# A Fourier layer and a mixture of experts on one core: the last-but-one batch's tokens made earlier, and the first head block turned at the last mix

## The chip, the cores and the metric

The kernel runs on one core of one Trainium2 chip. The metric is device microseconds of one execution. Before the change it is 1086.36 us, the median of 3 runs (1083.76, 1086.36 and 1087.21). The engines are named as in the profile: PE multiplies matrices, DVE is the vector engine, ACT the scalar engine, POOL the general engine that also issues the scatters, SP issues the other transfers.

## The reference

```python
X = np.fft.rfft(x, axis=1)                      # x: 8 batches x 2496 x 256
Yr = Xr @ w_r - Xi @ w_i + b_r
Yi = Xr @ w_i + Xi @ w_r + b_i
Y* = sign(Y*) * maximum(abs(Y*) - 0.01, 0)      # soft threshold, both parts
y = np.fft.irfft(Y, n=2496, axis=1)             # 19968 tokens of 256
do = y @ w_skip > 0                             # about half of the tokens
e = argmax(y[do] @ w_gate); g = softmax weight of e     # 8 experts, one each
out = y;  out[do] = y + g * (relu(y @ w1[e]) @ w2[e])   # w1 256x1024, w2 1024x256
```

All of it is in fp32. A product of two fp32 matrices is made as three products of parts (high by high, high by low, low by high), so most tensors exist twice, as a high part from ACT and a low part from DVE or POOL.

## The kernel before

The sequence is split as 39 by 64. A batch is worked off in 20 frequency steps, and the 8 batches make 160 steps in one straight program; every engine runs its instructions in the order in which the code issues them, and nothing else reorders them. Step `i` of the main loop belongs to batch `b` and frequency `k`. In this order it issues:

- `flush_y` and one output unit of the batch before (see below), then the inverse step `inv2_step` of frequency `i-4` (PE `pi`, L606; its copy `g` on ACT);
- the delayed pieces of work that are due at "inv2", and one step of the routing (`run_later`);
- the complex products `mix` (PE `pm`, L570). An odd step ends a pair of frequencies: DVE adds the bias to `pm` (L582), ACT makes `rl` (L584), DVE makes the two `y` (L590) of which the inverse is taken. An even step ends with `mix_sum`, whose products need `fl`, the low part of a sum that POOL makes (L552);
- the delayed work that is due at "sum", and `fwd2_step` for frequency `i+3` (PE `pb`, L536; `fh`, `im`, `fl`, `s`);
- a second output unit in the steps named in `KX` (in the last batch `KX7`), up to two scatters from the list `scq`, loads, and in the last batch a piece of the split of expert 0's weights (`wa2l`, L184).

An output unit makes 117 tokens; a batch has 21 of them, numbered 0 to 20, and besides a few other output tasks (a copy `gq`, a left-over unit, an ending). A unit has a first half, `t` (two transposing matmuls, L620 and L621, then ACT `th` L624 and DVE `tl` L625), and a second half, `y` (three matmuls, L632 to L634, then `row` and `lg` on ACT, L635 and L638). The second half is issued one unit later, by `flush_y`. Seven units are a chunk, and a chunk is followed by a routing of five parts, one part a call of `run_later`: the largest logit and the exponentials; a search for the expert; its one-hot matrix `oh`; a count on PE (`pr`, L675 and L677); and the places `pos` on DVE (L686 to L690). After them seven scatters `xs<-row,pos` of POOL (L693) send the chunk's tokens to the lists of their experts. Batch `b`'s units are made during batch `b+1`. The chunks of batch 6 are numbered 0, 7 and 14 by their first unit and 6, 13 and 20 by their last.

Behind step 159 come four steps (160 to 163) that hold only the last inverse steps, the output units that are left, and one head block task each (`fill.pop`). A head block is a block of 256 tokens of expert 0, from a list that is already full: three of them are worked off while batch 7's tokens are made. A block is loaded as `xg` by SP (L222), turned (`turn`: DVE transpose `hxt<-xg` L229, ACT `bxh` L232, DVE `bxl` L233), then goes through eight `up` tasks (PE `hph`, L241, six matmuls each) and eight `down` tasks (PE `pos`, L254). Then, in the tail, batch 7's own 24 output tasks follow with a head block task behind every third, the first of them `t_0`; SP loads the next expert's weights (`ws`, 2 MB, L172) ahead of it. Behind the tail the experts' loops run to the end.

Of the kernel before, what the change touches and what calls it, by code (L numbers as in the profile page):

```python
# [17 lines left out]
F32 = mybir.dt.float32  # L18
# [8 lines left out]
B, S, D = 8, 2496, 256  # L27
# [9 lines left out]
BLK = 256  # L37
# [3 lines left out]
HEAD = ((3, 6),)  # L41
NHEAD = sum(n for n, _ in HEAD)
D_SUM, D_RELU, D_Y0, D_Y1 = (1, "inv2"), (1, "inv2"), (1, "sum"), (1, "sum")
KX, KX7 = (0, 5, 9, 10, 12, 14, 18, 19), (0, 1, 2, 10, 12, 14, 19)
KA0 = (2, 4, 6, 8)
RK = (13, 15, 18, 3)
WLOAD, WST = (7, 11, 12, 15), (0, 0, 1, 0)
# [119 lines left out]
def load_quarter(nc, a, e, j, st):  # L167

    i, q = divmod(j, 2)
    src = a[("moe_w1", "moe_w2")[i]][e].rearrange("(c p) f -> p c f", p=128)  # L170
    at = (slice(None), slice(q, q + 1) if i == 0 else slice(4 * q, 4 * q + 4))
    nc.sync.dma_start(st.rearrange("p (c f) -> p c f", c=(1, 4)[i]), src[at])  # L172
# [17 lines left out]
def load_expert(nc, a, pool, e):  # L190

    t = pool.tile([128, K1 * D], F32, name=f"ws{e}", tag="g", bufs=2)
    st = [t[:, F * j : F * j + F] for j in range(4)]
    return st, [lambda j=j: load_quarter(nc, a, e, j, st[j]) for j in range(4)]
# [123 lines left out]
def fft_and_route(tc, a, out, zs, xs, kp, pp, keep_, outer):  # L318
# [6 lines left out]
    sp = es.enter_context(tc.tile_pool(name="sp", bufs=2, side="right", reuse_waits="tile"))  # L325
# [479 lines left out]
    def head_tasks(wt, pool):  # L805
        r2 = [sp.tile([128, F // 256, BLK], F32R, name=f"hhl{i}", tag="r", bufs=3) for i in range(2)]
        bk = Blocks(tc, out, xs, ident, pool, None, lambda f: r2[f // 4][:, f % 4, :], pp.tile([128, 2, D], F32, name="pos", tag="pm", bufs=2))

        def load(j):
            row = nc.values_load(  # L810
                hd["rows"][0:1, j : j + 1], engines=(mybir.EngineType.SP,), min_val=0, max_val=E * CAP,
                skip_runtime_bounds_check_because="a block of expert 0 or the padding",
            )
            hd["row"] = row
            sorted_rows(j, bk.load(row))
# [26 lines left out]
                sorted_rows(j, [bk.load_rows(hd["row"])])  # L842
                nxt()

        def first():
            bk.xt = sp.tile([128, 2 * BLK], F32, name="hxt", tag="rl", bufs=1)
            bk.turn()

        load(0)
        tasks = [first]  # L850
        for j in range(NHEAD - 1):
            for f in range(F // 128):
                tasks.append(lambda j=j, f=f: up(j, f, lambda: load(j + 1)))
# [34 lines left out]
    def run_later():  # L888
        if later and next(later[0], True):
            later.pop(0)  # L890
# [9 lines left out]
    def point(p):  # L900
        for f in slots.pop((now[0], p), []):
            f()
# [64 lines left out]
    steps = B * K1  # L967
    outq = []
    for i in range(steps + LAG):
        b, k = divmod(i, K1)  # L970
        if k == K1 - 2 and b + 2 < B:
            a1q += a1_tasks(b + 2)
        if i == 10:
            setup_c()
        now[0] = i
        flush_y()
        if outq:
            outq.pop(0)()
        if i >= LAG:
            inv2_step(*divmod(i - LAG, K1))  # L980
        point("inv2")
        run_later()
        point("route")
        if i < steps:
            mix(b, k)
        for _ in range(1 + (i in KA0)):
            a1_step(a1q)
        if i < steps and k % 2 == 0:
            mix_sum(b, k)
        point("sum")  # L990
        if i + AHEAD < steps:
            fwd2_step(*divmod(i + AHEAD, K1))
        if i >= steps:
            fill.pop(0)()
        if i >= LAG and (i - LAG) % K1 == K1 - 1:
            assert len(outq) == 0, len(outq)
            outq += out_tasks((i - LAG) // K1)
        if i >= steps:
            continue
        if len(outq) > 1 and k in (KX if b < B - 1 else KX7):  # L1000
            outq.pop(0)()
        for _ in range(2 if len(scq) > (4 if b < B - 1 else 1) else 1):
            if scq:
                scq.pop(0)()
        if k in RK[:3] and b + 1 < B:
            load_r(b + 1, RK.index(k))
        if k == RK[3] and b:
            load_r(b, 3)
        if b == B - 1 and k == 0:
            assert not a1q and not prepped  # L1010
            xes.close()
            wp = outer.enter_context(tc.tile_pool(name="wp", bufs=1, side="left", reuse_waits="tile"))
            wt = weight_tiles(wp, "wa")
            wsq, stages = [], {}
            hq = outer.enter_context(tc.tile_pool(name="hq", bufs=1, side="left", reuse_waits="tile"))
        if b == B - 1 and k in WLOAD:
            j = WLOAD.index(k)
            if WST[j] not in stages:
                stages[WST[j]] = sp.tile([128, KG * D], F32, name=f"stage{j}", tag="r", bufs=3)
            load_quarter(nc, a, 0, j, stages[WST[j]][:, :F])  # L1020
            wsq += split_quarter(nc, j, stages[WST[j]][:, :F], wt)
        if b == B - 1 and k in WSPLIT:
            wsq.pop(0)()
        if b == B - 1 and k == K1 - 2:
            bk, fill, last = head_tasks(wt, hq)
    ws, quarters = load_expert(nc, a, gp, 1)
    for f in quarters:
        f()
# [133 lines left out]
```

## Time and profile before

The profiled execution took 1084.19 us, of which the span of its instructions is 1082.4 us.

| Part of the program | us | what runs |
|---|---|---|
| up to step 142 | 0 to 483.0 | setup and batches 0 to 6 |
| steps 143 to 159 | 483.0 to 540.24 | the last batch's mixes |
| steps 160 to 163 | 540.24 to 554.96 | last inverse steps, first head block begins |
| tail | 554.96 to 632.12 | batch 7's tokens, three head blocks |
| experts | 632.12 to 1082.4 | eight loops |

Over the span PE is busy 1033.3 us (95%), DVE 727.6 (67%), ACT 604.5 (56%) and POOL 442.8 (41%), and the mean granted clock of PE is 0.988 of full speed. A row of a timeline is read as: when the instruction starts, how long it takes, what it writes from what, and in brackets how long its engine was idle before it and what released it. In a row of windows each engine has its busy time and the number of its instructions. Where two rows follow each other on an engine, the distance of their starts is what the first cost.

### The profile page before, as it was taken

How to read it: one execution, taken by the hardware profiler on the slowest of the kernel's cores; microseconds unless marked ns; L12 is line 12 of the kernel's file. 1: busy time of each engine (PE TensorE's matmuls, PEld its weight loads, DVE VectorE, ACT ScalarE, POOL GpSimd, SP SyncE). 2: the span in 40 equal slices, each digit the busy share in tenths (PEclk: the TensorE clock that was granted, in tenths of full speed). 3: DMA queues.
4: the chain of work that ended last, by engine and by line, in shares of the span. 5: the costliest groups of instructions: out<-in, count | busy, mean ns of one | idle time of the engine just before them, and what ended most of it. 6: DMA issues, size and time to landing. Idle time of an engine off the chain costs nothing. (4 is left out here: it accounts for less than half of the span.)

```text
span 1082.4 us, 27569 instructions
## 1 busy us (share of the span) xinstructions
PE 1033.3 (95%) x8412; PEld 1003.9 (93%) x8412; DVE 727.6 (67%) x2024; ACT 604.5 (56%) x1813; POOL 442.8 (41%) x602
## 2 busy tenths in 40 slices
PE   8999999999999999999977889999999999999997
PEld 7889999999999999999866889999899999999997
DVE  4688888888887888889954446465646546465643
ACT  5768788787886877866744234243434224243422
POOL 3524285582666838544455532222222222222222
PEclk9999999999999999999989999999999999999999
DMA  8655657567466756452563535242425225242221
GB/s 261 204 139 134 186 134 194 164 185 192 134 171 165 192 163 161 118 140 78 145 167 94 154 91 150 68 140 70 137 65 153 66 56 157 58 146 65 72 68 49
DMA packets 133041, 143.10 MB, mean 132 GB/s; under 512 B 57113, under 2 KB 116682, under 8 KB 132935
## 3 DMA queue, kind: packets, MB, share of 16 engines
q1 hardware_dynamic: 117941, 121.21, 41.4%
q0 software_dynamic: 14864, 20.55, 6.1%
q8 instruction: 51, 0.84, 0.3%
q14 instruction: 55, 0.45, 0.1%
q10 hardware_dynamic: 130, 0.05, 0.0%
HBM read 80.52 MB, written 72.07 MB: 141 GB/s over the span
## 5 line engine op out<-in xcount | busy, mean ns | idle before, releaser
L243 ACT ACTIVATE hh<-ph 128x256 fp32r<-128x256 f32 x304 | 110.4, 385 | 229.9 <-PE ph L241 134.7
L693 POOL DMA_INDIRECT xs<-row,pos x168 | 169.3, 1008 | 83.0 <-issue 41.4
L244 DVE SCALAR_TENSOR_TENSOR hl<-ph,hh 128x256 fp32r<-128x256 f32 x304 | 121.7, 422 | 73.4 <-ACT hh L243 54.0
L590 DVE SCALAR_TENSOR_TENSOR y<-pm,rl 64x256 f32<-64x256 f32 x320 | 134.2, 419 | 3.8
L552 POOL TENSOR_TENSOR fl<-s,fh 128x256 fp32r<-128x256 f32 x80 | 60.7, 759 | 163.1 <-issue 82.5
L570 PE MATMUL pm<-wh,fh 128*128 128x256 f32 x480 | 109.9, 310 | 2.2 <-DVE bias L558 1.2
L241 PE MATMUL ph<-bxh,wb1h 128*128 128x256 f32 x352 | 99.0, 281 | 5.4 <-PEq L1158 2.8
L536 PE MATMUL pb<-fwd,r 128*128 128x128 f32 (+1 forms) x640 | 98.9, 277 | 0.1
L570 PE MATMUL pm<-wh,fl 128*128 128x256 f32 x480 | 96.7, 282 | 2.2 <-POOL fl L552 1.6
L241 PE MATMUL ph<-bxl,wb1h 128*128 128x256 f32 x352 | 98.6, 280 | 0.0
L241 PE MATMUL ph<-bxh,wb1l 128*128 128x256 f32 x352 | 98.4, 279 | 0.0
L606 PE MATMUL pi<-inv,y 128*128 128x128 f32 (+1 forms) x640 | 98.1, 276 | 0.1
L570 PE MATMUL pm<-wl,fh 128*128 128x256 f32 x480 | 95.8, 281 | 0.0
L536 PEld LDWEIGHTS pb<-fwd,r 128*128 128x128 f32 (+1 forms) x640 | 87.0, 192 | 3.9 <-ACT r L436 0.5
L405 POOL TENSOR_TENSOR xl<-xr,xh 117x512 fp32r<-117x512 f32 x63 | 81.1, 1289 | 19.0 <-ACT xh L403 17.0
L625 DVE TENSOR_TENSOR tl<-pt,th 117x266 fp32r<-117x266 f32 x168 | 69.5, 427 | 28.7 <-ACT th L624 16.6
L606 PEld LDWEIGHTS pi<-inv,y 128*128 128x128 f32 x640 | 85.5, 192 | 0.7 <-ACT lg L638 0.3
L544 ACT ACTIVATE fh<-pb 128x256 fp32r<-128x256 f32 x160 | 61.6, 385 | 43.5 <-PE pb L536 33.7
L547 DVE TENSOR_TENSOR fl<-pb,fh 128x256 fp32r<-128x256 f32 x160 | 67.6, 422 | 26.2 <-ACT im L546 8.4
L570 PEld LDWEIGHTS pm<-wh,fh 128*128 128x128 f32 x480 | 76.0, 191 | 8.1 <-DVE bias L558 1.8
L270 POOL TENSOR_TENSOR idy<-idv,zero 128x2 int32<-128x2 int32 x32 | 6.0, 188 | 184.3 <-DVE idv L286 184.3
L624 ACT ACTIVATE th<-pt 117x266 fp32r<-117x266 f32 x168 | 68.4, 407 | 22.7 <-PE py L634 8.5
(221 smaller groups left out, 3221.5 us busy)
## 6 DMA issues: line engine op xcount, KB each, us to landing
out<-row SPq DMA_DIRECT2D x72, 273.0 KB
xr<-in_xc SPq DMA_DIRECT2D x21, 819.0 KB
zs<-z SPq DMA_DIRECT2D x63, 273.0 KB
r<-zs SPq DMA_DIRECT2D x49, 320.0 KB
ws<-in_moe_w SPq DMA_DIRECT2D x28, 512.0 KB
xres<-xs SPq DMA_DIRECT2D x41, 258.0 KB
xg<-xs SPq DMA_DIRECT2D x164, 64.0 KB, 1.9
xs<-row,pos POOLq DMA_INDIRECT x168
```

Source lines behind the costliest of these rows:

```text
L241: self.nc.tensor.matmul(p, l_[:, c, fc], r_[:, c, :], start=n == 0, stop=n == 5)
L243: self.nc.scalar.activation(self.hh[:, f, :], p, AF.Relu)
L244: self.nc.vector.scalar_tensor_tensor(out=self.hl(f), in0=p, scalar=0.0, in1=self.hh[:, f, :].bitcast(F32), op0=ALU.max, op1=ALU.subtract)
L405: eng.tensor_tensor(out=xl[:, :n], in0=v, in1=xh[:, :n].bitcast(F32), op=ALU.subtract)
L536: mm(pb[:, h], r[:kp_, kk, 128 * h : 128 * h + 128], fwd2[:kp_, k], start=True, stop=True)
L547: nc.vector.tensor_tensor(out=for_k(xl), in0=src, in1=for_k(xh).bitcast(F32), op=ALU.subtract)
L570: mm(out, flat(l_, h, j), r_[:, j, h], start=start and n == 0, stop=n == 5, skip_group_check=True)
L590: nc.vector.scalar_tensor_tensor(out=y[64 * c : 64 * c + 64], in0=t[rows, c], scalar=LAM, in1=r[rows, c], op0=ALU.add, op1=ALU.min)
L606: mm(pi[:, h, :nn], y[:, 128 * h : 128 * h + 128], inv2[:, k, :nn], start=True, stop=True)
L624: nc.scalar.activation(th[:np_], pt[:np_], AF.Copy)
L625: nc.vector.tensor_tensor(out=tl[:np_], in0=pt[:np_], in1=th[:np_].bitcast(F32), op=ALU.subtract)
L693: si = nc.gpsimd.indirect_dma_start(out=xs, out_offset=bass.IndirectOffsetOnAxis(ap=pos[pl, o : o + 1], axis=0), in_=row[pl, o, :], in_off ...
```

## The change

Three things are changed. The list `KX7`, the steps of the last batch with a second output unit, goes from seven entries to eleven, most of them early. In the last batch `run_later` is called a second time in every step, behind the delayed work of "sum". And the first head block is turned right behind step 159 instead of in step 160 as a head block task: its tile `hxt` now shares the tag `fh` and not `rl`, and the list of head block tasks is one task shorter, so that the steps 160 to 163 hold `up` 0 to 3 and not the turn and `up` 0 to 2.

```diff
-KX, KX7 = (0, 5, 9, 10, 12, 14, 18, 19), (0, 1, 2, 10, 12, 14, 19)
+KX, KX7 = (0, 5, 9, 10, 12, 14, 18, 19), (0, 1, 2, 3, 4, 5, 6, 7, 8, 11, 12)
...
-        def first():
-            bk.xt = sp.tile([128, 2 * BLK], F32, name="hxt", tag="rl", bufs=1)
-            bk.turn()
-
+        bk.xt = sp.tile([128, 2 * BLK], F32, name="hxt", tag="fh", bufs=2)
         load(0)
-        tasks = [first]
+        tasks = []
...
         point("sum")
+        if b == B - 1:
+            run_later()
         if i + AHEAD < steps:
             fwd2_step(*divmod(i + AHEAD, K1))
...
             wsq.pop(0)()
         if b == B - 1 and k == K1 - 2:
             bk, fill, last = head_tasks(wt, hq)
+        if i == steps - 1:
+            bk.turn()
```

How this moves the work is seen in each engine's order. On PE, from the end of the last mix (`pm_9`) to the first `up` (`hph_0`), the order before is as follows; the last number of a name only counts tiles.

```order
L570 MATMUL pm_9_9018<-wh,fl_9_8874 128x256 x2
L620 MATMUL pt_18_9097<-iw,g_7097 117x138
...
L632 MATMUL py_16_9110<-th_16_8995,i1h 117x266
...
L632 MATMUL py_17_9116<-th_17_9078,i1h 117x266
...
L620 MATMUL pt_19_9122<-iw,g_7097 117x138
...
L606 MATMUL pi_16_9129<-inv_96,y_16_9032 128x128 x2
L632 MATMUL py_18_9148<-th_18_9100,i1h 117x266
...
L620 MATMUL pt_20_9154<-iw,g_7097 117x138
...
L606 MATMUL pi_17_9161<-inv_96,y_17_9035 128x128 x2
...
L675 MATMUL pr_13_9165<-oh_13_9009,tri 117x56
...
L241 MATMUL hph_0_9174<-bxh,wa1h 128x256
```

There stand three `t` (18 to 20), three of five `y` (16 to 18; 19 and 20 follow behind `hph_0` and `hph_1`), and the count `pr` of batch 6's middle chunk. After the change the same place holds this.

```order
L570 MATMUL pm_9_9130<-wh,fl_9_9014 128x256 x2
L632 MATMUL py_20_9179<-th_20_9093,i1h 117x266
...
L606 MATMUL pi_15_9188<-inv_96,y_15_9065 128x128 x2
...
L570 MATMUL pm_9_9130<-wh,fl_9_9014 128x256 x2
L606 MATMUL pi_16_9220<-inv_96,y_16_9144 128x128 x2
L241 MATMUL hph_0_9235<-bxh,wa1h 128x256
...
L606 MATMUL pi_17_9252<-inv_96,y_17_9147 128x128 x2
...
L675 MATMUL pr_20_9256<-oh_20_9197,tri 117x56
...
L241 MATMUL hph_1_9265<-bxh,wa1h 128x256
```

All `t` and `y` of batch 6 now stand ahead of the end of the last mix, as does the middle chunk's count; the last chunk's count comes behind `hph_0`, where before it stood behind `t_0` and the left-over unit of batch 7. On DVE, around the last bias addition, the order before is this (`t_13` to `row_7` are the routing of batch 6's middle chunk).

```order
L659 SCALAR_TENSOR_TENSOR t_13_9007<-d_13_9005,pack 117x56
L660 TENSOR_REDUCE mx_13_9008<-t_13_9007 117x7
L661 TENSOR_REDUCE s_13_9010<-ex_13_9006 117x7
L582 TENSOR_TENSOR pm_9_9018<-pm_9_9018,bias 128x512
L625 TENSOR_TENSOR tl_18_9101<-pt_18_9097,th_18_9100 117x266
L625 TENSOR_TENSOR tl_19_9126<-pt_19_9122,th_19_9125 117x266
L663 SCALAR_TENSOR_TENSOR mx_13_9008<-lg_7_8598,mx_13_9008 117x7
L666 TENSOR_SCALAR s_13_9010<-s_13_9010 117x7
L667 TENSOR_TENSOR oh_13_9009<-t_13_9007,mx_13_9008 117x56
L668 RECIPROCAL row_7_8597<-s_13_9010 117x7
...
L229 STREAM_TRANSPOSE hxt<-xg 128x512
L233 TENSOR_TENSOR bxl<-hxt,bxh 128x8x2x32
```

After the change the same place holds this (`t_20` to `row_14` are the routing of the last chunk).

```order
L582 TENSOR_TENSOR pm_9_9130<-pm_9_9130,bias 128x512
L659 SCALAR_TENSOR_TENSOR t_20_9195<-d_20_9193,pack 117x56
L660 TENSOR_REDUCE mx_20_9196<-t_20_9195 117x7
L661 TENSOR_REDUCE s_20_9198<-ex_20_9194 117x7
L229 STREAM_TRANSPOSE hxt<-xg 128x512
L233 TENSOR_TENSOR bxl<-hxt,bxh 128x8x2x32
L663 SCALAR_TENSOR_TENSOR mx_20_9196<-lg_14_8792,mx_20_9196 117x7
L666 TENSOR_SCALAR s_20_9198<-s_20_9198 117x7
L667 TENSOR_TENSOR oh_20_9197<-t_20_9195,mx_20_9196 117x56
L668 RECIPROCAL row_14_8791<-s_20_9198 117x7
L590 SCALAR_TENSOR_TENSOR y_18_9229<-pm_9_9130,rl_9_9213 64x256 x2
L590 SCALAR_TENSOR_TENSOR y_19_9232<-pm_9_9130,rl_9_9213 64x256 x2
```

The transpose stands nine instructions behind the bias addition before and four behind it after, now ahead of the routing's `oh` and of `y_18` and `y_19`; no `tl` stands in between any more. On POOL, in the last batch's steps, the scatters stand between the low parts `fl_3` to `fl_7` before as follows (`row_7_7448` and `row_14_7757` are the last two chunks of batch 5).

```order
L552 TENSOR_TENSOR fl_3_8208<-s_3_8209,fh_3_8207 128x2x128
L693 DMA xs<-row_7_7448,pos_13_8126 162048x258 x2
...
L693 DMA xs<-row_7_7448,pos_13_8126 162048x258 x2
L552 TENSOR_TENSOR fl_4_8295<-s_4_8296,fh_4_8294 128x2x128
L693 DMA xs<-row_7_7448,pos_13_8126 162048x258 x3
L552 TENSOR_TENSOR fl_5_8402<-s_5_8403,fh_5_8401 128x2x128
L693 DMA xs<-row_14_7757,pos_20_8329 162048x258 x2
L552 TENSOR_TENSOR fl_6_8510<-s_6_8511,fh_6_8509 128x2x128
L693 DMA xs<-row_14_7757,pos_20_8329 162048x258 x4
L552 TENSOR_TENSOR fl_7_8624<-s_7_8625,fh_7_8623 128x2x128
```

After the change they stand in this order (`row_0_8252` and `row_7_8507` are the first two chunks of batch 6).

```order
L693 DMA xs<-row_7_7448,pos_13_8089 162048x258 x4
L552 TENSOR_TENSOR fl_3_8245<-s_3_8246,fh_3_8244 128x2x128
L693 DMA xs<-row_7_7448,pos_13_8089 162048x258
L693 DMA xs<-row_14_7757,pos_20_8225 162048x258 x3
L552 TENSOR_TENSOR fl_4_8368<-s_4_8369,fh_4_8367 128x2x128
L693 DMA xs<-row_14_7757,pos_20_8225 162048x258 x2
...
L693 DMA xs<-row_14_7757,pos_20_8225 162048x258 x2
L552 TENSOR_TENSOR fl_5_8500<-s_5_8501,fh_5_8499 128x2x128
...
L693 DMA xs<-row_0_8252,pos_6_8560 162048x258 x4
L552 TENSOR_TENSOR fl_7_8758<-s_7_8759,fh_7_8757 128x2x128
...
L693 DMA xs<-row_7_8507,pos_13_8885 162048x258 x4
L552 TENSOR_TENSOR fl_9_9014<-s_9_9015,fh_9_9013 128x2x128
```

Four scatters stand between two low parts, ahead of `fl_4` and `fl_7`, before; after, they stand ahead of `fl_3`, `fl_4`, `fl_5`, `fl_7` and `fl_9`. Behind `fl_9` there are 21 scatters of batch 6 before (three chunks) and ten after (three of the middle chunk and the last chunk's seven).

On SP the stores `out<-row` of batch 6's last chunk stand behind the load of the second head block before and ahead of it after; that load still waits for the first block's turn, and the weight load `ws` comes next in both.

## Rows read from the trace of the kernel before

**Rows 1.** Busy time per engine in four stretches: from, to, length; then PE, PEld, DVE, ACT, POOL.

```profile
483.00:520.61 37.61, 35.97 (x306) 34.64 (x304) 34.52 (x116) 25.01 (x82) 19.01 (x22) 1.00 0.37 104
520.61:540.24 19.63, 18.33 (x151) 17.53 (x152) 17.44 (x54) 15.79 (x52) 5.76 (x8) 1.00 0.45 128
540.24:554.96 14.72, 11.22 (x71) 10.46 (x69) 9.71 (x30) 7.52 (x24) 7.87 (x11) 0.77 0.36 82
554.96:632.12 77.16, 61.55 (x461) 57.35 (x459) 32.98 (x132) 26.05 (x96) 40.59 (x51) 0.93 0.52 148
```

**Rows 2.** Timeline of PE, one step: start us, us, engine, line; bracket is idle before.

```profile
532.73 0.37 PE L632 MATMUL py<-th,i1h 117*117 117x266 f32 x1
...
533.18 0.40 PE L620 MATMUL pt<-iw,g 128*117 128x138 f32 x2
...
533.65 0.60 PE L606 MATMUL pi<-inv,y 128*128 128x128 f32 x4
534.01 0.48 PE L570 MATMUL pm<-wh,fh 128*128 128x256 f32 x2
```

**Rows 3.** Timeline of PE, a count of routed tokens and what follows it.

```profile
557.44 0.19 PE L675 MATMUL pr<-oh,tri 117*117 117x56 bf16 x1
...
557.84 0.47 PE L620 MATMUL pt<-iw,g 128*117 128x138 f32 x2
```

**Rows 4.** The page's line for the split of a transposed output tile on DVE.

```profile
L625 DVE TENSOR_TENSOR tl<-pt,th 117x266 fp32r<-117x266 f32 x168 | 69.5, 427 | 28.7 <-ACT th L624 16.6
```

**Rows 5.** Timeline of PE, from the last mix's end to the last batch's first tile.

```profile
540.24 0.40 PE L620 MATMUL pt<-iw,g 128*117 128x138 f32 x2
...
547.96 0.58 PE L241 MATMUL hph<-bxh,wa1h 128*128 128x256 f32 x1 [2.46 <-issue]
...
549.28 0.42 PE L241 MATMUL hph<-bxh,wa1h 128*128 128x256 f32 x1
...
554.35 0.28 PE L241 MATMUL hph<-bxl,wa1h 128*128 128x256 f32 x1
...
554.96 0.49 PE L620 MATMUL pt<-iw,g 128*117 128x138 f32 x2
```

**Rows 6.** Timeline of DVE around the first turn.

```profile
542.12 0.20 DVE L659 SCALAR_TENSOR_TENSOR t<-d,pack 117x56 f32<-117x56 f32 x1
...
542.61 0.69 DVE L582 TENSOR_TENSOR pm<-pm,bias 128x512 f32<-128x512 f32 x1
...
546.53 0.71 DVE L229 STREAM_TRANSPOSE hxt<-xg 128x512 f32<-128x512 f32 x1
547.94 0.69 DVE L233 TENSOR_TENSOR bxl<-hxt,bxh 128x512 fp32r<-128x512 f32 x1 [0.69 <-issue]
```

**Rows 7.** Timeline of ACT around the first turn.

```profile
547.28 0.63 ACT L232 ACTIVATE bxh<-hxt 128x512 fp32r<-128x512 f32 x1 [2.55 <-issue]
```

**Rows 8.** Timeline of POOL, a sum's low part behind four scatters.

```profile
502.87 0.73 POOL L552 TENSOR_TENSOR fl<-s,fh 128x256 fp32r<-128x256 f32 x1
```

**Rows 9.** Timeline of PE, the sum that waits for it.

```profile
503.65 0.50 PE L570 MATMUL pm<-wh,fl 128*128 128x256 f32 x2 [0.74 <-POOL fl L552]
```

**Rows 10.** Timelines of SP, POOL, ACT and PE in the tail's first stall.

```profile
556.87 4.76 SPq L172 DMA_DIRECT2D ws<-in_moe_w  x4
...
560.53 1.00 POOL L693 DMA_INDIRECT xs<-row,pos  x1 [0.30 <-issue]
...
562.77 0.76 ACT L624 ACTIVATE th<-pt 117x266 fp32r<-117x266 f32 x2 [4.75 <-remote]
...
563.68 0.38 PE L241 MATMUL hph<-bxh,wa1h 128*128 128x256 f32 x1 [3.45 <-DVE tl L625]
```

**Rows 11.** Busy time in two-microsecond stretches of that stall; PEclk, DMA share and GB/s end each row.

```profile
560.00:562.00 2.00, 0.23 (x2) 0.00 (x0) 0.00 (x0) 0.00 (x0) 1.22 (x2) 1.00 0.92 272
564.00:566.00 2.00, 2.00 (x13) 2.00 (x12) 1.75 (x8) 1.11 (x6) 0.54 (x1) 0.61 1.04 320
566.00:568.00 2.00, 2.00 (x11) 2.00 (x10) 0.73 (x4) 0.85 (x5) 1.44 (x2) 0.53 0.86 291
```

## Prediction

> **What bounds the kernel now.** First the windows of busy time by stretch [rows 1]. In steps 143 to 153 (483.00 to 520.61 us) PE is busy 35.97 of 37.61 us and DVE 34.52: PE sets the pace, with 1.64 us of idle time, and DVE is close behind. In steps 154 to 159 (520.61 to 540.24) it is 18.33 and 17.44 of 19.63. In the four steps behind the last mix (540.24 to 554.96) PE has only 11.22 of 14.72 us, at a mean granted clock of 0.77. In the tail it has 61.55 of 77.16, which is 15.6 us of idle time. The work behind the tail is not touched, so the sum is made up to 632 us.
>
> Then the timeline of PE around the last mix [rows 5]. The last mix ends at 540.24; I call this T0. Batch 6's leftover units fill PE for some five microseconds, PE then waits 2.46 us, and the first `up` starts at 547.96, which is T0+7.7. The first tile of batch 7 (`t_0`) starts at 554.96, T0+14.7. The wait's cause stands in the rows of DVE and ACT [rows 6, 7]: the bias addition runs at 542.61 (DVE is 2.4 us behind PE), the transpose only at 546.53, behind two `tl`, four routing operations and two `y`; `bxh` starts at 547.28. So the first stretch behind T0 waits for the turn, the mixes wait for PE with DVE close by, and the tail is full of holes.
>
> **The change, part by part.** Prices from PE's rows: a `y` is 533.18 - 532.73 = 0.45 us, a `t` 533.65 - 533.18 = 0.47 [rows 2], a count 557.84 - 557.44 = 0.40 [rows 3]; on DVE a `tl` is 0.43 [rows 4].
>
> *(a) T0 comes later.* Three `t`, five `y` and one count go from behind T0 to ahead of it. They are not spread evenly: the new list has six more units up to step 153 and fewer after it. Up to there PE gets 6 x 0.47 + 6 x 0.45 + 0.40 = 5.9 us more. Of the 1.64 us of idle time I give back 1.0, which leaves +4.9. From there to T0 three `t` and one `y` less are 1.9 us; DVE loses three `tl` (1.3 us) and six small routing operations in that stretch, where it was as full as PE, so that PE's time should really go: -2.0. Six units sooner is 2.6 us more of `tl` on DVE in a stretch where it had 34.52 of 37.61; with the stretch 4.9 us longer it still fits.
>
> POOL has a price here too. Behind four scatters a low part `fl` started at 502.87 [rows 8], and the sum's product that needs it had waited 0.74 us on PE when it started at 503.65 [rows 9]; with slower matmuls around the wait I put it at 1.0. Four scatters stand ahead of an `fl` five times instead of twice. With two units a step the steps are also longer by 0.92 us, which gives the scatters more time, so I take 0.8 us for all three new ones; the ends are 0 and 3 x 1.0. Moved into the main loop, the count waits for `oh` of DVE, with the scatters queued on POOL behind its places; by the same cover (PE's mixes stand ahead of the count in a step) I take nothing.
>
> T0 moves by +4.9 - 2.0 + 0.8 = +3.7 us. The ends: +5.9 - 1.64 - 1.9 - 1.3 = +1.1 if all idle time of the two stretches is used up, and +5.9 - 1.9 + 3.0 = +7.0 if none is and each new burst costs 1.0.
>
> *(b) From T0 to the first tile of batch 7.* Before, the three routing operations from 542.12 on and a `tl` stood ahead of the bias addition [rows 6]; after, two small ones do, so it comes about 0.5 us sooner, at T0+1.9, and costs 0.6. The three routing operations (542.61 - 542.12 = 0.49) now follow, then the transpose; from its start to that of `bxh` it was 547.28 - 546.53 = 0.75 and from there to the first `up` 547.96 - 547.28 = 0.68 [rows 5 to 7]. The first `up` starts at T0 + 1.9 + 0.6 + 0.5 + 0.75 + 0.7, about T0+4.4, rather than T0+7.7. The tile `hxt` changes its place in memory; the place's last reader is a mix, which is done by then. PE has only one inverse step (534.01 - 533.65 = 0.36 [rows 2]) in these 4.4 us. Behind it stand four `up`, three inverse steps and a count. At full clock the last five matmuls of an `up` took 554.96 - 554.35 = 0.61 us [rows 5], so an `up` of six takes 0.73, and the sum is 4 x 0.73 + 3 x 0.36 + 0.40 = 4.4 us.
>
> What the clock does here decides. [...] At full clock throughout it would be T0+4.4+4.4 = T0+8.8, or -5.9; if the turn is no earlier, 0. [...]
>
> *(c) The count in the tail.* The last chunk's count no longer stands behind `t_0`: -0.4 us. Its DVE part goes too, where DVE has time (32.98 of 77.16 us [rows 1]): nothing. The end of the tail (last count, places, scatters, load, turn) is the same in order and gets nothing.
>
> *(d) The first stall of the tail.* PE stood still for 3.45 us up to 563.68, with ACT idle for 4.75 us up to 562.77 [rows 10], while the expert weights were coming in (issued from 556.87 on, 4.76 us for issuing) and POOL ran seven scatters in a row, the last at 560.53. In 560 to 562 nothing but POOL was at work, and the DMA engines were busy for a share of 0.92 [rows 11]. Behind the stall the clock fell to 0.61 and 0.53 for 4 us: 2 x 0.39 + 2 x 0.47 = 1.7 us. In the changed kernel this train of seven belongs to a chunk that is done ahead of T0 but for three; the last chunk's train comes in its place about 6 us earlier against `t_0`; the second train disappears from the tail. The weight load no longer waits for the stores of the last chunk and is issued behind the first `up`, about T0+6.5 by this sum instead of T0+16.6 (556.87), so most of it is done when the place of the stall is reached. I take the stall and its half clock as gone: -5.15. The ends: 0 (it stays) and -8.6, if the train that leaves the tail altogether frees as much again (3.45) out of the tail's 15.6 us of idle time.
>
> The sum: +3.7 - 2.7 - 0.4 - 5.15 = -4.55 us. On the profiled execution (1084.19 us, of which 1082.4 are its span) that is 1079.6. That execution is 2.2 us below the median of the runs (1086.36), so against the median it is 1081.8.
>
> **The rivals.**
> *The stall stays.* It could hang on something other than these transfers and scatters, such as the place in ACT's program: from `t_0` on ACT's instructions are the same and as many stand ahead of them. Or the transfers now collide with the inverse steps ahead of `t_0`. For it: ACT waited for nothing that the profile names ("remote"). Against it: the DMA share of 0.92 and 1.04 just there [rows 11]. Then the sum is +3.7 - 2.7 - 0.4 = +0.6, or 1087.0: no change. [...]
>
> *The scatters hold up the sums (slower).* One mechanism: in steps 143 to 159 five low parts `fl` stand behind four scatters each, and PE's sum waits for each of them. Seen so far is 1.0 us for one. If DVE also falls back by as much as it is behind at T0 (2.4 us), the scatters start that much later and a wait can be 0.74 + 2.4 = 3.1 us. In the middle it is 2.0, and five of them are 10 us instead of the 0.8 in the sum: -4.55 + 9.2 = +4.65, or 1091.0. The sign turns at a mean wait of 1.1 us (5 x 1.1 is about 0.8 + 4.55). For it: DVE at 92% in that stretch. Against it: longer steps.
>
> *The turn comes no earlier.* DVE has to finish what is queued ahead of the bias addition, and with the units moved ahead this could be more than before. Then (b) is 0, the wait is longer than before, and the sum without (d) is +3.7 - 0.4 = +3.3, or 1089.7.
>
> **How the numbers follow.** A measurement of this kernel tells 0.3% (3.3 us) from no change, that is, below 1083.1 and above 1089.6. The forecast has a chance of 0.42, its own range 1078.3 to 1084.4 (from the end of (d), 3.5 below, to four fifths of the way to the upper end of (a), 2.6 above), and four fifths of it are faster than the bound. The stall that stays has 0.32, nearly all within the bound. The scatters have 0.18, mostly slower, and the turn that comes no earlier 0.08. This gives faster 0.38, same 0.39, slower 0.23. The range reaches from 1078.0 to 1090.5.
>
> **What the changed profile would show.** (a) The last mix ends near 543.9, and rows of PE in the last batch wait for `fl` under 1 us. (b) The transpose is followed by the first `up` some 4.4 us behind the last mix's end, with matmuls of 0.42 us, and `t_0` starts some 12.0 us behind it, near 555.9. (d) Between `t_0` and the next 10 us PE has no gap above 1 us, and the weight load is issued ahead of `t_0`. From `t_0` to the first expert loop it takes about 71.6 us and not 77.16. The forecast is wrong if this stretch stays above 75 us, if T0 comes later than 547.5, or if waits for `fl` add up to over 5 us.

## The result: 0.5% slower, and the profile after

| | median us | runs us |
|---|---|---|
| before | 1085.42 | 1083.76, 1084.48, 1086.36, 1087.21 |
| after | 1091.25 | 1089.49, 1090.65, 1091.85, 1092.58 |

The ratio is 1.0054 (95% interval 1.0029 to 1.0078); a fourth run of the kernel before puts its median at 1085.42, not 1086.36. The forecast was 1081.8 us; the time lies just over the range's end (1090.5) and on the other side of the kernel before. The profiled execution took 1089.49 us, its span 1087.7.

The windows of the changed kernel's profile, by the same program stretches as [rows 1] (the first begins at the forward products of frequency 3, in step 140, which in the kernel before started at 482.42, 0.6 us ahead of the first row there; the prediction and the table of stretches count that row's first step two too high):

```profile
479.23:533.72 54.49, 46.53 (x361) 45.41 (x359) 41.11 (x136) 29.30 (x101) 25.88 (x29) 0.91 0.35 97
533.72:552.68 18.96, 16.32 (x138) 15.70 (x137) 16.46 (x50) 15.01 (x47) 9.78 (x11) 1.00 0.40 107
552.68:565.32 12.64, 8.63 (x50) 8.09 (x48) 8.39 (x27) 4.36 (x11) 2.78 (x5) 0.73 0.85 244
565.32:638.77 73.45, 61.96 (x446) 59.42 (x445) 32.02 (x120) 25.72 (x94) 35.16 (x46) 0.86 0.42 119
```

The first of them in the kernel before, from the same place on:

```profile
482.42:520.61 38.19, 36.55 (x311) 35.22 (x309) 34.90 (x116) 25.01 (x82) 19.03 (x22) 1.00 0.36 102
```

The stretch up to step 153 is 54.49 us long, where it was 38.19; the next one 18.96 (19.63), the one from the last mix to batch 7's first tile 12.64 (14.72), the tail 73.45 (77.16). From the forward products of step 137, here before and after, to the end of the last mix (540.24 and 552.68) it was 69.16 us and is 85.91: +16.75, not +3.7.

```profile
471.08 0.71 PE L536 MATMUL pb<-fwd,r 64*128 64x128 f32 x4
```

```profile
466.77 0.71 PE L536 MATMUL pb<-fwd,r 64*128 64x128 f32 x4
```

PE's idle time in the first two rows is 10.6 us, where it was 2.9, and the granted clock of the first is 0.91, where it was 1.00. The last mix ends far later than forecast; what lies behind it is shorter, if by less than forecast (2.1 and 3.7 us, not 2.7 and 5.55). (Up to step 137, where both programs are alike, this execution happens to be 4.3 us shorter than that of before, and behind the tail 1.4 us.)

Where PE waits, from its timeline in the changed kernel (idle time and releaser in brackets):

```profile
485.00 0.19 PE L675 MATMUL pr<-oh,tri 117*117 117x56 bf16 x1 [2.75 <-DVE oh L667]
...
495.44 0.55 PE L570 MATMUL pm<-wh,fl 128*128 128x256 f32 x2 [2.16 <-POOL fl L552]
...
518.64 0.21 PE L675 MATMUL pr<-oh,tri 117*117 117x56 bf16 x1 [2.13 <-DVE oh L667]
...
538.48 0.19 PE L675 MATMUL pr<-oh,tri 117*117 117x56 bf16 x1 [1.05 <-DVE oh L667]
...
550.82 0.51 PE L570 MATMUL pm<-wh,fl 128*128 128x256 f32 x2 [1.53 <-POOL fl L552]
...
557.08 0.49 PE L241 MATMUL hph<-bxh,wa1h 128*128 128x256 f32 x1 [3.77 <-ACT bxh L232]
```

Three counts `pr` wait for their one-hot matrix `oh`, 2.75, 2.13 and 1.05 us, and two sums wait for `fl`, 2.16 and 1.53 us. Before, one wait for `fl` of 0.74 us stood there [rows 9], and one for `oh`:

```profile
490.64 0.19 PE L675 MATMUL pr<-oh,tri 117*117 117x56 bf16 x1 [0.34 <-DVE oh L667]
```

The last row of the changed kernel is the first `up`, 4.40 us behind the last mix's end at 552.68, as the prediction had it. DVE's timeline ahead of the first of the counts:

```profile
479.77 1.74 DVE L590 SCALAR_TENSOR_TENSOR y<-pm,rl 64x256 f32<-64x256 f32 x4
481.52 0.21 DVE L654 TENSOR_REDUCE m<-lg 117x7 f32<-117x56 f32 x1
...
482.74 0.42 DVE L547 TENSOR_TENSOR fl<-pb,fh 128x256 fp32r<-128x256 f32 x1 [0.76 <-ACT im L546]
...
483.28 0.21 DVE L659 SCALAR_TENSOR_TENSOR t<-d,pack 117x56 f32<-117x56 f32 x1
...
484.74 0.22 DVE L667 TENSOR_TENSOR oh<-t,mx 117x56 bf16<-117x56 f32 x1
```

The two `y` of a pair (four instructions, 1.74 us) run first, then the routing's first, second and third part within 3.4 us, with other work of DVE and one wait between them. That wait of 0.76 us is for ACT, and comes from the routing as well. Its exponentials `ex` stand on ACT ahead of the step's `fh` and `im`, and need `d`, which DVE makes behind the four `y`; ACT stood idle for 3.00 us:

```profile
482.02 0.25 ACT L656 ACTIVATE ex<-d 117x56 f32<-117x56 f32 x1 [3.00 <-DVE d L655]
```

PE had reached the count at 482.25 and stood until 485.00. Behind the wait the windows show the clock:

```profile
484.00:486.00 2.00, 0.99 (x11) 0.99 (x11) 1.66 (x7) 1.24 (x4) 0.68 (x1) 0.88 0.76 185
486.00:488.00 2.00, 2.00 (x11) 2.00 (x10) 0.00 (x0) 0.00 (x0) 0.00 (x0) 0.50 0.86 235
488.00:490.00 2.00, 2.00 (x16) 2.00 (x15) 1.69 (x5) 0.89 (x3) 0.00 (x0) 0.77 0.88 237
```

The last three columns are clock, DMA share and GB/s: 0.50 for the two microseconds behind the wait, 0.77 in the next.

### The profile page after: what moved, and what is told of

Same layout as the page of the kernel before. It is cut to its first block, busy times and chain, and to the rows that moved or that the text cites. A ratio compares the mean times of both kernels' runs of the same rounds, so it can differ in the third digit from the quotient of the medians.

```text
span 1087.7 us, 27553 instructions
## 1 busy us (share of the span) xinstructions
PE 1036.0 (95%) x8412; PEld 1008.5 (93%) x8412; DVE 729.9 (67%) x2024; ACT 604.4 (56%) x1813; POOL 442.7 (41%) x602
## 5 line engine op out<-in xcount | busy, mean ns | idle before, releaser
L544 ACT ACTIVATE fh<-pb 128x256 fp32r<-128x256 f32 x160 | 61.7, 386 | 56.1 <-PE pb L536 43.1
L570 PEld LDWEIGHTS pm<-wh,fh 128*128 128x128 f32 x480 | 76.3, 192 | 7.6 <-ACT fh L551 1.7
L608 ACT ACTIVATE g<-pi 128x256 f32<-128x256 f32 x152 | 76.6, 504 | 7.9 <-PE pb L536 2.5
```

The lines of the kernel that those rows point to most:

```text
L570: mm(out, flat(l_, h, j), r_[:, j, h], start=start and n == 0, stop=n == 5, skip_group_check=True)
L608: nc.scalar.activation(g[:, :, :, 2 * k - 1 : 2 * k + 1], pi.rearrange("p h (s r) -> p h s r", r=2), AF.Copy)
```

## The experiments

The runs fell on several chips. Beside the same kernel before, which took 1054 us on some and 1085 to 1092 us on the others, each ratio is of runs on one chip. The table has the ratio to the kernel before, and from one profile of each: the mixes (step 137's forward products to the last mix's end), the way from there to batch 7's first tile, and from that to the first expert loop.

| kernel | before, us | ratio (95%) | mixes | to tile | tail |
|---|---|---|---|---|---|
| before, again | 1092 | - | 71.4 | 16.4 | 82.9 |
| after, again | 1092 | 1.0039 (1.0012 to 1.0065) | 86.6 | 12.9 | 76.0 |
| after, no early turn | 1092 | 1.0047 (1.0025 to 1.0070) | 85.9 | 13.0 | 76.3 |
| after, route twice from step 7 | 1092 | 1.0002 (0.9980 to 1.0023) | 80.5 | 12.3 | 77.9 |
| before, third | 1054 | - | 66.2 | 13.8 | 57.1 |
| after, third | 1054 | 1.0166 (1.0142 to 1.0191) | 79.3 | 12.6 | 61.7 |
| before + second routing point | 1054 | 1.0109 (1.0079 to 1.0139) | 77.1 | 12.7 | 57.4 |
| the same + filler on PE | 1054 | 1.013 (one run) | 76.6 | 12.7 | 57.6 |
| after, empty part ahead of count | 1054 | 1.0092 (1.0068 to 1.0117) | 78.6 | 10.5 | 62.8 |
| after, second point at step's end | 1054 | 1.0139 (1.0113 to 1.0166) | 80.6 | 11.0 | 60.2 |
| after, from step 7, empty part | 1054 | 1.0113 (1.0084 to 1.0143) | 75.8 | 11.4 | 60.1 |
| even units, one routing point | 1054 | 1.0025 (1.0005 to 1.0044) | 68.0 | 12.4 | 60.9 |
| early turn alone | 1054 | 1.0020 (1.0006 to 1.0033) | 66.2 | 13.3 | 61.0 |
| early turn, second time | 1054 | 1.0023 (1.0011 to 1.0036) | 66.2 | 13.3 | 61.9 |
| early turn, third time | 1053 | 1.0011 (0.9998 to 1.0024) | 66.2 | 13.3 | 61.0 |
| early turn + empty task | 1087 | 1.0013 (0.9995 to 1.0032) | 70.2 | 13.3 | 83.3 |
| even units + empty task | 1087 | 1.0021 (1.0005 to 1.0037) | 72.3 | 11.8 | 85.8 |
| early turn + empty task, again | 1053 | 0.9967 (0.9953 to 0.9981) | 66.2 | 13.3 | 56.9 |

**The second routing point alone**

```diff
 # the kernel before
         point("sum")
+        if b == B - 1:
+            run_later()
```

> Only the second routing point is added to the kernel before; the units stay at their old steps and the first turn in step 160. Theory (the count): with two routing parts a step the count on PE stands one or two parts behind the one-hot matrix on DVE, so PE waits for it at each count of the last batch's steps (2 to 3 us at each of three, and half clock behind each, about 2 us more). The last mix should end 8 to 14 us later against step 140, and the time be 5 to 10 us over the kernel before. Rival (two units a step crowd DVE and POOL): without the earlier units nothing is crowded, no wait for the one-hot matrix above 1 us, and the time is within 2 us of the kernel before.

The mixes are 77.1 us, 10.9 over the 66.2 of before, and the ratio 1.0109: no earlier unit and no early turn is needed for most of the loss (the time is 11.9 us over, where 5 to 10 were expected; the whole change has mixes of 79.3 us on such a chip). PE, then POOL of this kernel:

```profile
481.59 0.21 PE L675 MATMUL pr<-oh,tri 117*117 117x56 bf16 x1 [2.75 <-DVE oh L667]
...
482.89 0.63 PE L570 MATMUL pm<-wl,fh 128*128 128x256 f32 x2
...
492.39 0.80 PE L570 MATMUL pm<-wh,fl 128*128 128x256 f32 x2 [2.15 <-POOL fl L552]
```

```profile
489.28 1.00 POOL L693 DMA_INDIRECT xs<-row,pos  x1 [8.01 <-DVE m L654]
490.59 0.99 POOL L693 DMA_INDIRECT xs<-row,pos  x1 [0.30 <-issue]
491.60 0.74 POOL L552 TENSOR_TENSOR fl<-s,fh 128x256 fp32r<-128x256 f32 x1
```

The first count waits the same 2.75 us, and `pm` behind it takes 0.63 us a pair. The places come sooner than before, so two scatters now stand on POOL ahead of the `fl` at 491.60, and the sum waits 2.15 us for it. So the waits for `fl` come from the routing too. (The earlier units without a faster routing were not tried: a chunk's rows have three buffers, which the units would fill ahead of the scatters that empty them.)

**Filler work in the wait**

```diff
 # the second routing point alone, and
+        if key == "5_13":
+            spin(6)
         pr = bank(pp, "pr" + key)
```

> The second routing point alone (as in the first run of these), with six matmuls of no use on PE just ahead of the middle chunk of batch 5's count, where PE had waited 2.75 us. Theory (the wait costs twice, once as a wait and once by the clock behind it): with PE at work in the wait the clock stays at full, so the mix behind the count takes 0.24 us a pair of matmuls and not 0.43; from the forward products of frequency 5 to those of frequency 6 the stretch falls from 7.2 us to about 5 us. Rival (half clock has another cause there): the matmuls behind the count stay at 0.63 us.

```profile
479.92 2.76 PE L350 MATMUL pw<-pad 128*128 128x256 f32 x12
482.93 0.21 PE L677 MATMUL pr<-oh,tri 117*117 117x56 bf16 x1 [0.25 <-DVE oh L667]
...
483.67 0.40 PE L570 MATMUL pm<-wl,fh 128*128 128x256 f32 x2
```

With PE at work up to the count, the pair of matmuls behind it takes 0.40 us and not 0.63, and from one step's forward products to the next's around the count (frequencies 4 and 5, which the expectation counts one too high) it is 5.81 us, where it was 7.22 and, in the third profile of before, 2.67. So of the 4.55 us that this count cost (its own 0.40 among them), 1.4 were the slower matmuls' behind it, where the changed kernel's window shows a clock of 0.50: this wait was paid a second time. All mixes together gained only half a microsecond (77.1 to 76.6), since the sums and counts behind it still waited.

**The second point only from the seventh step on**

```diff
-        if b == B - 1:
+        if b == B - 1 and k >= 6:
             run_later()
```

> The changed kernel, with the second routing point only from the last batch's seventh step on. Theory (the count): the first long wait for the one-hot matrix (2.75 us), the wait for the low part right behind it (2.16 us) and the half clock behind both go, while the later ones stay; the last mix ends 6 to 9 us earlier against step 137 than in the changed kernel and the time is 5 to 9 us under it. Rival (units crowd DVE and POOL): the early steps gain nothing, the time is within 3 us of the changed kernel.

The mixes fall from 86.6 to 80.5 us, and the time to that of the kernel before: 2.7 us under the changed kernel, where 5 to 9 were expected. The first count waits only 0.32 us, and behind the longest of the waits that the counts still have the clock stays at 1.00. What is left is the same thing later, on PE and on DVE:

```profile
526.12 0.24 PE L675 MATMUL pr<-oh,tri 117*117 117x56 bf16 x1 [2.61 <-issue]
```

```profile
523.90 1.72 DVE L590 SCALAR_TENSOR_TENSOR y<-pm,rl 64x256 f32<-64x256 f32 x4
...
525.85 0.22 DVE L667 TENSOR_TENSOR oh<-t,mx 117x56 bf16<-117x56 f32 x1
```

The count waits 2.61 us for an `oh` that stands behind `y`. The clock did not fall behind this wait, so it is not every wait of this length that is paid twice (clock, DMA share and GB/s end the row):

```profile
526.00:528.00 2.00, 1.88 (x20) 1.88 (x21) 1.99 (x7) 0.42 (x1) 0.55 (x1) 1.00 0.10 29
```

**Where the parts stand in a step**

```diff
 # (1) one empty part ahead of the count, in the last three batches
-        if b == B - 1:
+        if b >= B - 3:
             yield
 # (2) second point at the end of the step
-        point("sum")
-        if b == B - 1:
-            run_later()
...
+        if b == B - 1:
+            run_later()
         if len(outq) > 1 and k in (KX if b < B - 1 else KX7):
 # (3) second point from the seventh step on, empty part in the last two batches
```

> The changed kernel, with one empty routing part between the one-hot matrix and the count, in the last three batches. Theory (the count): PE's waits for the one-hot matrix in the last batch fall below 0.5 us each, the half clock behind them goes, the last mix ends 6 to 10 us earlier against step 140 than in the changed kernel, and the time is 1081 to 1086. Rival (units crowd DVE and POOL): the waits turn up at another instruction (low part of the sum, or tl), the last mix ends within 3 us of the changed kernel's, and the time is 1089 to 1093.

> The changed kernel, with the second routing point at the end of the step instead of ahead of the forward products. Theory (the count): where the one-hot matrix is made at the first point and counted at the second, a mix now lies between and PE does not wait; where it is the other way round PE still waits. So one or two of the three waits go and the time is between, 1085 to 1089. Rival (units crowd DVE and POOL): 1089 to 1093, with waits for the low part of the sum.

> The changed kernel with the second routing point from the seventh step on and an empty routing part between the one-hot matrix and the count for batches 6 and 7. Theory (the count behind a busy DVE): the waits for the one-hot matrix that were left (1.25, 2.61 and 0.96 us) fall below 1 us in sum, the last mix ends 3 to 5 us earlier against step 137 than with the seventh step alone (80.5 us), and the time is 0.2 to 0.5% under the kernel before. Rival (DVE is full there): the waits move to other instructions, the last mix gains under 1.5 us, and the time is within 0.2% of the kernel before or over it.

All three missed. Against the changed kernel's 79.3 us the mixes are 78.6, 80.6 and 75.8. In the first, the count's wait fell from 2.75 to 1.11 us, but a mix now waited 1.41 us for the bias and a sum 1.80 for `fl`; in the second a count still waited 3.02, though `ex` stands behind the step's `fh` and `im` there; in the third counts waited 1.72 and 1.11. (The ratios, 1.0092, 1.0139 and 1.0113, are nevertheless under the 1.0166 of the changed kernel, in part by the first tile, which comes 10.5 to 11.4 us behind the last mix and not 12.6.) The waits move rather than go: with two routing parts a step DVE's queue is what is late, wherever the count is put. So the count is where PE meets it, and the rival's "crowded DVE" has a share of the loss that these runs do not put a number on.

**Evenly spread units without the second point**

```diff
 # the changed kernel
-KX7 = (0, 1, 2, 3, 4, 5, 6, 7, 8, 11, 12)
+KX7 = (0, 1, 2, 5, 7, 9, 11, 13, 15)
-        if b == B - 1:
-            run_later()
```

> The changed kernel without the second routing point, with the second units spread over the last batch (steps 0, 1, 2, 5, 7, 9, 11, 13 and 15): two more than before, evenly. Theory (the second routing point is the loss, units that are spread cost only their work): no wait for the one-hot matrix above 1 us, the last mix ends 1.5 to 4 us later than before against step 137, batch 7's first tile 2 to 3.5 us sooner behind it, the tail a few us shorter; time 0.1 to 0.4% under the kernel before. Rival (two units a step crowd DVE and POOL wherever they are): waits for the low part or the row buffers above 2 us in sum, time 0.2% or more over the kernel before.

The mixes are 68.0 us, +1.8, without a wait for `oh` over 0.32, and the first tile comes 1.4 us sooner behind them: both stretches are as the theory had them (the tile's gain a little under), and units that are spread cost their work only. But the time is 0.25% over and not under, because the tail, which should have been shorter, is 3.8 us longer than the 57.1 of before. The early turn, which this kernel has too, shows why.

**The early turn, alone and taken away**

```diff
 # alone: the kernel before with the diff's parts on hxt, first() and bk.turn()
 # taken away: the kernel before with the new KX7 and the second run_later()
```

> The changed kernel without the turn's move: earlier units and the second routing point alone. Theory (the early turn shortens the stretch from the last mix to batch 7's first tile when the units are gone from there): the first up starts 1.5 to 3 us later than in the changed kernel, and the time is 1 to 4 us over it. Rival (the turn does nothing or costs): within 1 us of the changed kernel or under it.

> Only the first turn is moved to the last mix; units and routing as before. Theory: the mixes are untouched, so the last mix ends where it did against step 140 (within 1 us); the first up starts about 5 us behind it instead of 7.7, with the old units filling PE in between, and the first tile of batch 7 comes 2.5 to 5 us earlier. Time 2 to 5 us under the kernel before. Rival (the turn is not what the first up waits for, or the inverse steps' y are now late instead): the first tile comes within 1 us of where it did, and the time is the same.

> The early turn alone, once more, beside a profile of the kernel before on the same chip. Theory from the first run of it: the first up starts about 3 us sooner behind the last mix, but batch 7's first tile under 1.5 us sooner, and the time is within 0.3% of the kernel before. Rival (what it gains ahead of the first tile is kept): 0.2 to 0.4% under the kernel before.

Taken away, the first `up` starts 6.8 us behind the last mix instead of 4.4, but the first tile at 13.0 instead of 12.9, with one `up` less ahead of it: in that stretch the rival's case. The times decide nothing: the ratios, 1.0047 and 1.0039, overlap, and the medians are 4.2 us apart. Alone, the first `up` comes 3.0 us sooner, the tile 0.5 (with one `up` more ahead of it), and the time is 0.1 to 0.2% over in each of three runs (with the third below, which is within its noise). The tails differ by 4 us, and here is why. PE and DVE with the early turn alone:

```profile
571.14 0.21 PE L675 MATMUL pr<-oh,tri 117*117 117x56 bf16 x1 [2.21 <-DVE row L668]
...
573.69 0.63 PE L254 MATMUL pos<-wa2l,hh 128*128 128x256 f32 x2
```

```profile
568.58 0.70 DVE L229 STREAM_TRANSPOSE hxt<-xg 128x512 f32<-128x512 f32 x1
...
570.78 0.22 DVE L667 TENSOR_TENSOR oh<-t,mx 117x56 bf16<-117x56 f32 x1
```

The same places in the kernel before on the same chip:

```profile
569.25 0.19 PE L675 MATMUL pr<-oh,tri 117*117 117x56 bf16 x1
```

```profile
568.59 0.22 DVE L667 TENSOR_TENSOR oh<-t,mx 117x56 bf16<-117x56 f32 x1
...
570.23 0.70 DVE L229 STREAM_TRANSPOSE hxt<-xg 128x512 f32<-128x512 f32 x1
```

The list of head block tasks is one task shorter, so each later task stands one place earlier in the tail. The second block's turn thereby moves on DVE from behind the `oh` of batch 7's middle chunk to ahead of it. The count waits 2.21 us for it, and the block's `pos` matmuls behind it run at 0.63 us a pair, where the kernel before has 0.40.

**The empty task**

```diff
 # the early turn alone, and one empty head block task ahead of the tail
+        tasks.insert(4, lambda: None)
```

> The early turn alone, with one empty head block task at the tail's start, so that the later tasks (the second block's turn among them) stand at the tail places of the kernel before. Theory (the list that is one task shorter moves the second turn on DVE ahead of a one-hot matrix, whose count then waits 2.2 us and half clock follows): the wait goes, the stretch from batch 7's first tile to the first expert loop falls by 3.5 to 5 us against the early turn alone, and the time is 0.2 to 0.5% under that kernel, that is 0.25% under to level with the kernel before. Rival (the early turn costs elsewhere, as by its tile's new place): the time stays 0.2% over the kernel before.

> The evenly spread units and the early turn without the second routing point, with the same empty task. Theory: as for the run beside it, 0.2 to 0.5% under the same kernel without the empty task, which stood 0.25% over the kernel before; level with the run beside it within 0.15%. Rival: 0.25% over the kernel before.

> The early turn with the empty head block task once more, beside the early turn alone on the same chip. Where the kernel before takes about 1054 us the count's wait is on the path, and theory (the shift of the second turn) puts this kernel 0.2 to 0.5% under the early turn alone and 0.25% under to level with the kernel before; where it takes about 1088 us the tail's stalls hide it and both are within 0.2% of the kernel before. Rival: no difference between the two on either.

> The early turn alone, for the comparison on the same chip: 0.2% over the kernel before where that takes about 1054 us.

On the chip of 1087 us both are level with or just over the kernel before, which decides nothing, since the tail is 83 us there. On the chip of 1053 us the tail is 56.9 us, against 61.0 with the early turn alone on the same chip, and the time is 0.33% under the kernel before (ratio 0.9967, 0.9953 to 0.9981), where the early turn alone is at 1.0011. The turn stands behind the `oh` again, and the count no longer waits:

```profile
567.78 0.22 DVE L667 TENSOR_TENSOR oh<-t,mx 117x56 bf16<-117x56 f32 x1
...
569.41 0.70 DVE L229 STREAM_TRANSPOSE hxt<-xg 128x512 f32<-128x512 f32 x1
```

The window of its tail, without a clock under 1.00:

```profile
544.20:601.07 56.87, 52.44 (x454) 51.80 (x453) 33.16 (x131) 26.54 (x95) 42.45 (x52) 1.00 0.70 202
```

This is the only version that came out under the kernel before, and on that chip only. The empty task gives back the tail's 4 us. But of the some 3.4 us that the profile has less than that of the kernel before, from step 137 on, only 0.2 are the tail's and 0.5 the first tile's; 2.7 are in the expert loops (446.8 and 449.5 us), and no run shows why.

**The kernels again on other chips**

> The kernel before once more, for its profile on the chip of these runs. No theory tells it apart; the last mix should end about 69 us behind step 137's forward products, as in the first profile of before.

> The changed kernel once more, on the same chip as the runs beside it. Both theories: 0.4 to 1.0% over the kernel before.

> The kernel before, once more for its profile. If the tail's stalls (3.45 us at the first) belong to the chip and not to the program, they are there where the kernel before takes about 1090 us and missing where it takes about 1054 us, and the stretch from batch 7's first tile to the first expert loop is about 77 to 83 us on the one and 57 to 62 us on the other. If they belong to the program, they are there on both.

> The changed kernel, once more. If the kernel before takes about 1090 us here, 0.4 to 0.6% over it, as measured twice. If it takes about 1054 us, the tail has no stall that could go, so that nothing of the 16 us that the mixes lose comes back there: 1.0 to 1.5% over it. Rival (the loss has the same size on every chip): 0.4 to 0.6% on both.

Where the kernel before takes 1054 us, its tail is this:

```profile
544.91:602.01 57.10, 52.92 (x460) 52.56 (x459) 33.54 (x132) 26.91 (x96) 41.21 (x51) 1.00 0.70 200
```

PE is idle 4.2 us of 57.1 (3.65 of them just ahead of the expert loops), where [rows 1] has 15.6 of 77.16, and there is no stall like that of [rows 10]. The change is 1.66% slower there (1.0 to 1.5% had been expected), 0.39 to 0.54% elsewhere. So the tail's stalls do not come from the program alone, which speaks against the rival that ties them to a place in ACT's program. They go with the chip, as far as one occasion on each chip can tell, and only where they are did the change shorten the tail.

## Why the prediction was wrong

The step that failed is in (a): "the count waits for `oh` of DVE ... I take nothing", with the reason that mixes stand ahead of the count. Three counts waited, 5.9 us in sum. For the first, no mix stands between: its `oh` is issued at the second routing point of a step and the count at the first point of the next, with only forward products, an output unit and an inverse step between them. For the other two a mix does stand between, and does not cover. The mix ahead of the count at 518.64 took PE about 1 us, and DVE came to the `oh` only 1.8 us behind its end (PE, then DVE):

```profile
515.56 0.48 PE L570 MATMUL pm<-wh,fh 128*128 128x256 f32 x2
```

```profile
518.27 0.22 DVE L667 TENSOR_TENSOR oh<-t,mx 117x56 bf16<-117x56 f32 x1
```

The time of DVE from `m` to `oh` was never worked out, only its load (34.52 of 37.61 us), and a load below 1 says nothing of how late one instruction is. The same part took 0.8 us for waits for `fl`, which measured 3.7 (and it counts 1.0 us for one such wait as seen, where [rows 9] has 0.74).

The term measured +16.75, outside its own ends of +1.1 and +7.0; on the two other chips with profiles of both kernels it was +15.2 (71.4 to 86.6) and +13.1 (66.2 to 79.3). By the rows it is made up so: 5.9 - 1.9 = 4.0 us of moved work, as forecast; 2.75 + 2.13 + 1.05 = 5.9 of counts that wait; 2.16 + 1.53 = 3.7 of sums that wait for `fl`; 0.8 of a wait for ACT's part of an output unit; some 4.9 by the clock in the first window ((1 - 0.91) x 54.49); and less the 2.9 us of idle time that was there before: 16.4. Of the signs of being wrong that the prediction names, one came: the last mix's end lies behind 547.5. The tail is under 75 us, and the waits for `fl` add up to less than 5.

- The 1.9 us that the last steps should have lost with their units, with DVE's relief 2.0: they lost 0.7, with 2.6 us of waits inside.
- (b) came near in number: the first `up` at T0+4.4 as worked out, first tile -2.1 us for -2.7. That term was the author's estimate of what a slow clock behind the wait costs, and no run shows it by itself; in its place the profiles show a granted clock of 0.51 for 6.39 us behind the wait of 2.46 us before (547.96 to 554.35) and of 0.51 for 6.90 us behind the wait of 3.77 us after (557.08 to 563.98). But the run without the early turn shows the first tile at the same place (13.0 and 12.9, with 16.4 for the kernel before on that chip), so it was not the turn that gave the 2.1, and that the number fits is in part luck. The second routing point alone had the tile at 12.7, where the whole change had 12.6 and the kernel before 13.8 on such chips; how the gain divides is not shown.
- (c) and (d), -5.55 together, were -3.7 on the first chip and -6.9 on the next (82.9 to 76.0). The stall was not gone: in place of PE's gap of 3.45 us, 8.7 us behind the first tile, there is one of 2.08 us at 8.9, and the tail's clock fell from 0.93 to 0.86 on the first chip:

```profile
574.22 0.55 PE L632 MATMUL py<-th,i1h 117*117 117x266 f32 x1 [2.08 <-ACT lgq L638]
...
595.02 0.27 PE L675 MATMUL pr<-oh,tri 117*117 117x56 bf16 x1 [2.23 <-PE py L634]
...
613.07 0.19 PE L675 MATMUL pr<-oh,tri 117*117 117x56 bf16 x1 [2.21 <-DVE oh L667]
```

  The weight load came at T0+6.7 as worked out (6.5), but the last train of scatters began at T0+12.2, not six microseconds sooner against the tile. The second row is the count of batch 7's middle chunk, which the shifted turn delays as it does with the early turn alone; the third is the last chunk's. I had seen the shift by one place in the order and had looked only at PE's side of it. Where the tail has no stall the same term is +4.6 (57.1 to 61.7).
- The rival of the scatters gave 1091.0 and the time is 1091.25, but its mechanism was a third of it: 3.7 us of waits for `fl`, not 10. That the sums meet is luck.

What stays open: what the tail waits for on the chips of 1085 to 1092 us (ACT's "remote"); what many units early in the batch cost without the second routing point; how the loss of the routing divides between late counts and a late DVE; and why the expert loops are about 2 us shorter with the early turn (446.6 to 448.3 us in five profiles of the early turn with or without the empty task, 449.5 to 450.3 in three of the kernel before).

## What to carry to other kernels

Where an engine is to take a product early, work out when the engine that makes it gets to it: the queue ahead of that one instruction, not the mean load (DVE's 34.52 of 37.61 us said nothing of the 2.75 us that a count waited). A second step of a pipeline per round makes the distance between producer and consumer half as long, and a wait on TensorE can be paid again by the clock behind it, as the 2.75 us were (clock 0.50 behind them) and the 2.61 us were not (1.00). The queues of two engines can hang together: an operation that waits on ACT also holds up what stands behind it there (`ex` had ACT idle for 3.00 us, and DVE then waited 0.76 us for the `im` behind it). When a task leaves a list that is dealt out by position, look what each later task now stands ahead of, on every engine: here an empty task in its place was worth more (the tail 56.9 us, not 61.0) than the move itself (the first tile 0.5 us sooner).

## What the runs showed of the hardware

One program differed by 3 to 4% from one chip to another, each used on one occasion (1049 to 1061 us on four, 1082 to 1097 on the others), mostly in the stretch with trains of scatters beside large loads (57 against 77 to 83 us), while its expert loops took 449.5 to 450.3 us on both kinds. Behind filler matmuls of 2.76 us and a count that PE then waited 0.25 us for, a pair of matmuls took 0.40 us, where it took 0.63 us behind a wait of 2.75 us; behind the same wait in the changed kernel the clock fell to 0.50. A wait's length alone does not tell: behind one of 2.61 us (the second point from the seventh step on) the clock stayed at 1.00, and behind one of 1.11 us (the same with an empty part) it fell to 0.50, with single matmuls `py` of 0.43 us that otherwise took 0.28.
